# Attention in chunks and an MLP on one Trainium2 core: V, scores and attention output by halves of a tile from the fifth tile on, and the last stores in eight transfers

## The chip, the cores and the metric

The kernel runs on one core of a Trainium2 chip. The metric is the time of one execution on the device in microseconds (us), taken as the median of several runs. A core has several engines that work side by side and wait for each other by semaphores: TensorE (PE in the profile, with PEld for its weight loads), VectorE (DVE), ScalarE (ACT), GpSimd (POOL), and SyncE (SP), which here only issues transfers. Sixteen DMA engines move data between the device's memory and the on-chip memory.

## The reference: what is computed

Eight batches of eight heads with 576 positions of 64 numbers go through attention within chunks of 64 positions, and the result through a two-layer MLP with an exact GELU:

```python
scores = scale * np.matmul(q_c, k_c.transpose(0, 1, 2, 4, 3))   # within each chunk of 64
attn = softmax(scores)                                          # over the 64 keys
out = np.matmul(attn, v_c)
x = out.transpose(0, 2, 1, 3).reshape(4608, 512)
h = x @ w_in                                                    # 512 x 2048
return gelu(h) @ w_out                                          # 2048 x 512
```

## The kernel before, in words

**Tiles.** A batch has nine chunks. The first eight (512 positions, `MT`) of batch t make tile t, for t = 0 to 7. The ninth chunks of all eight batches make a ninth tile, t = 8 (`B` in the code). Each tile has 512 rows of x. A tile goes through loads, casts to bf16 on GpSimd, scores, softmax, attention output (AV), x with the 512 features on the partitions, the first MLP product (`mm1_groups`), and the second (`mm2_seven` from tile 3 on, otherwise `mm2_slot`).

**Order.** The whole order is written out by hand. `phase(t, ...)` runs the MLP of tile t. Into it are hung, at named places (words of a written program in the first product, numbered places in the second), the steps of later tiles: scores of tile t+2 and AV and x of tile t+1 in the second product, and the issue of loads still further ahead. Each engine executes its own queue in that order, and SP's queue holds nearly all loads, all transposes by DMA and all stores but half of the last ones.

**From tile 4 on** (`FIRSTX = 4`) the attention goes as follows.

- `load_v_rows` (L113) loads V as 256-byte runs, one for each key and head, into a tile of 128 partitions x 8 heads x 4 slots. Heads of even and odd number are placed differently: `place(r, i)` (L148) gives for chunk i and head parity r the half of the partitions (0 or 1) and the slot. An even head has chunk i in half i % 2, an odd one in the other half. So a tile of the first eight takes four transfers for the even heads (128 KB each) and five for the odd ones (three of 128 KB and two of 64 KB), and tile 8, whose chunks come from eight batches, takes eight for each parity (64 KB each).
- `cast_v_rows` (L198) casts V on GpSimd in two steps, one for each head parity, into a tile with one more column, which holds ones, so that AV also gives the sums of the softmax.
- `quad_S` (L222) computes the scores: 64 products of 64x64 for a tile. The array of PE works as four quarters; a product occupies a half of the rows (the head parity r) and a half of the columns (o = c ^ r, with c the parity of the chunk). There are four banks of results, one for each pair of head groups and c. ScalarE takes the exponential of each bank.
- `rows_av` (L316) computes AV with the positions on the partitions: 64 products of 64 x 65. They lie in six banks: block b = (head group, pair of chunks) from 0 to 15, seven blocks in a bank, and a bank for each head parity. The sixth bank is borrowed from the second MLP product (`last`, the bank Z).
- `rows_x` (L333) divides on DVE, bank by bank (a reciprocal at L346 and a product at L348), and SP transposes the result into x by DMA, in two pieces (L340): blocks 0 to 6 after the first two banks, blocks 7 to 15 after all six.

**Around it.** `x_blocks` (L593) splits x into four blocks (two halves of the features, two halves of the positions) for a scheme with seven products in place of eight; `x_sums` (L597) makes four differences of them on DVE. In `mm1_groups` (L632) the word `p` stands for a plain block of four products with 512 columns (L685); from tile 3 on only tile 8 has such blocks, four of them.

**Loads around V of the last tiles.** During phase 5 SP issues the first part of tile 7's V, the transposes of x, a store, the second part of tile 7's V, the eight loads of tile 8's queries (L111), a store and the eight loads of tile 8's keys (L106). During phase 6 follow the transposes of tile 8's queries and keys (L187), for which GpSimd's casts (L154) must be done, and V of tile 8.

**The end.** `last_seven` (L794) computes the second product of tile 8. Its first half of the rows is stored by four transfers (two blocks m of 128 rows, two chunks each), its second half by eight (two column halves, two blocks, two chunks). In `store_rows` (L822) the even chunk's store goes out on SP and the odd one's on ScalarE's queue, so each issues six.

## Time and profile before

| | us |
|---|---|
| median of three runs | 272.89 (272.04 to 274.34) |
| profiled execution | 272.8 |
| its span, first to last instruction | 271.0 |
| TensorE busy | 260.0 (96% of the span) |
| VectorE, ScalarE, GpSimd busy | 199.6, 186.7, 76.8 |

The granted clock of TensorE was 0.996 of full speed in the mean over the span. The DMAs moved 56.60 MB at 209 GB/s in the mean. Times in rows of the profile are counted from the start of the span. In a row of a time order the first number is the start and the second the length in us; a bracket at the end gives the idle time of the engine just before and what ended it. The queue of an engine's issues has a q behind its name (SPq, ACTq). A row of a group has the count, the busy time, the mean in ns, and the idle time before it.

### The profile page before, as it was taken

The page shows a single profiled execution, that of the slowest core. Times are in us where ns is not written, and L with a number is a line of the kernel's source. Part 1 is how long each engine was busy: PE and PEld are TensorE (multiplying, and loading weights), DVE is VectorE, ACT ScalarE, POOL GpSimd, SP SyncE. Part 2 cuts the span into 40 slices and gives each one's busy share as a digit, 9 for nine tenths or more (in the row PEclk, how much of TensorE's full clock was granted, in tenths as well). Part 3 has the DMA queues.
Part 4 walks back from the last instruction along what each step waited for, and adds up shares of the span by engine and source line. Part 5 has one row for each costly group of instructions (what it writes and reads, how often), then busy time and mean ns, then how long its engine had stood idle before and what let it go on. Part 6 is the DMA issues. An engine that isn't in the chain of part 4 may idle for free.

```text
span 271.0 us, 7549 instructions
## 1 busy us (share of the span) xinstructions
PE 260.0 (96%) x3063; PEld 194.5 (72%) x3080; DVE 199.6 (74%) x368; ACT 186.7 (69%) x363; POOL 76.8 (28%) x127
## 2 busy tenths in 40 slices
PE   7989999999999999999999999999999999999990
PEld 3454454486458644888888888888888888887780
DVE  2673786979998789599669956985897589756930
ACT  3467756897767968895699579947994797259400
POOL 2635658361351151342036003610132011000000
PEclk9999999999999999999999999999999999999998
DMA  6999999998969998998999999996699560530014
GB/s 203 252 344 405 396 400 242 255 283 208 323 162 210 255 228 196 268 253 126 204 263 233 231 192 257 256 192 153 214 221 194 132 186 20 119 116 2 0 33 126
DMA packets 127523, 56.60 MB, mean 209 GB/s; under 512 B 103936, under 2 KB 121344, under 8 KB 127488
## 3 DMA queue, kind: packets, MB, share of 16 engines
q1 hardware_dynamic: 127008, 55.59, 81.7%
q10 hardware_dynamic: 480, 0.52, 0.8%
q8 instruction: 24, 0.39, 0.6%
q14 instruction: 11, 0.09, 0.1%
HBM read 36.70 MB, written 9.44 MB: 170 GB/s over the span
## 4 chain that ended last, share of the span: by engine, by line
PE 80%; SPq 9%; DMA 5%; issue 1%; POOL 1%; ACT 0%; DVE 0%; POOLq 0%
PE y_ps L730 20%; PE h_Y L663 12%; PE y_ps L844 11%; PE h_Z L663 8%; PE h_X L663 8%; PE h_ps L523 5%; PE y_ps L869 4%; PE y_ps L739 3%; PE h_ps L685 2%; DMA arrival<-in_moe_w_in_dram 2%; SPq L139 2%; SPq L106 2%; SPq L111 2%; PE s_ps L232 2%; DMA k_t<-k_nat 1%
## 5 line engine op out<-in xcount | busy, mean ns | idle before, releaser
L663 PEld LDWEIGHTS <-w_in_s 128*128 128x128 bf16 x464 | 45.3, 98 | 6.1
L663 PEld LDWEIGHTS <-w_in_sb 128*128 128x128 bf16 x348 | 34.0, 98 | 6.8 <-issue 0.5
L154 POOL CAST q_nat<-arrival 128x512 bf16<-128x512 f32 x33 | 19.4, 627 | 47.4 <-DMA arrival<-in_q_dram 47.1
L663 PE MATMUL h_X<-x,w_in_sb 128*128 128x256 bf16 x232 | 32.6, 272 | 0.0
L844 PE MATMUL y_ps<-w_out_sb,h 128*128 128x512 bf16 x137 | 31.7, 379 | 0.9 <-issue 0.8
L730 PEld LDWEIGHTS <-h_s 128*128 128x128 bf16 x304 | 29.7, 98 | 3.4
L663 PE MATMUL h_Y<-x_t,w_in_s 128*128 128x256 bf16 x232 | 31.8, 272 | 0.0
L730 PEld LDWEIGHTS <-h 128*128 128x128 bf16 x288 | 27.9, 98 | 3.6
L206 POOL CAST v_nat<-arrival 128x1024 bf16<-128x1024 f32 x14 | 15.2, 1098 | 50.9 <-DMA arrival<-in_v_dram 50.8
L154 POOL CAST k_nat<-arrival 128x512 bf16<-128x512 f32 x34 | 21.7, 673 | 22.5 <-DMA arrival<-in_k_dram 20.5
L730 PE MATMUL y_ps<-w_t,h_s 128*128 128x256 bf16 x208 | 24.8, 273 | 0.0
L844 PEld LDWEIGHTS <-h 128*128 128x128 bf16 x144 | 13.4, 98 | 15.0 <-issue 0.2
L730 PE MATMUL y_ps<-w_out_sb,h 128*128 128x256 bf16 x192 | 22.9, 273 | 0.0
L941 ACT ACT_TABLE_LOAD x16 | 20.5, 1283 | 1.0 <-PEq L1161 0.7
L670 ACT ACTIVATE h<-h_Y 128x512 bf16<-128x512 f32 x29 | 17.1, 594 | 2.0 <-PE h_Y L663 1.6
L698 ACT COPY h_Y<-h_X 128x512 f32<-128x512 f32 x29 | 16.5, 583 | 2.8 <-PE h_X L663 2.6
L670 ACT ACTIVATE h<-h_X 128x512 bf16<-128x512 f32 x29 | 17.2, 596 | 1.4 <-PE h_X L663 0.8
L663 PE MATMUL h_Z<-x_t,w_in_s 128*128 128x256 bf16 x116 | 17.4, 273 | 0.0
L663 PE MATMUL h_Z<-x_t,w_in_sb 128*128 128x256 bf16 x116 | 16.9, 272 | 0.0
L663 PE MATMUL h_Y<-x,w_in_s 128*128 128x256 bf16 x116 | 16.9, 273 | 0.0
L239 ACT ACTIVATE pT<-s_ps 128x512 bf16<-128x512 f32 x28 | 14.5, 601 | 2.7 <-PE s_ps L232 2.7
L709 DVE COPY h_a<-h_Y 128x512 f32<-128x512 f32 x8 | 5.5, 692 | 14.5 <-PE h_Y L663 14.5
(145 smaller groups left out, 492.0 us busy)
## 6 DMA issues: line engine op xcount, KB each, us to landing
arrival<-in_q_dram SPq DMA_DIRECT2D x7, 1024.0 KB
arrival<-in_k_dram SPq DMA_DIRECT2D x24, 256.0 KB
out_dram<-y_sb SPq DMA_DIRECT2D x22, 256.0 KB
arrival<-in_v_dram SPq DMA_DIRECT2D x42, 128.0 KB
arrival<-in_moe_w_out_dram SPq DMA_DIRECT2D x4, 1024.0 KB
out_dram<-y_sb SPq DMA_DIRECT2D x5, 512.0 KB
arrival<-in_v_dram SPq DMA_DIRECT2D x8, 256.0 KB
arrival<-in_moe_w_in_dram SPq DMA_DIRECT2D x4, 512.0 KB
```

The lines of the kernel that those rows point to most:

```text
L154: copy(st[nm][:, g].rearrange("p j r d -> p r j d"), st[nm + "f"][:, 2 * g:2 * g + 2])
L206: copy(st["v"][:, r::2, :, :D], st["vf"][:, r::2])
L239: nc.scalar.activation(pT[:].rearrange("p u (c j) -> p u c j", j=J), s_ps[g2][c][:].rearrange("p u (j c) -> p u c j", j=J), Act.Exp, scale ...
L523: nc.tensor.matmul(h_ps[a][:], w_in_sb[:, ks, f * P:(f + 1) * P], st["x"][:, ks, :], start=(ks == 0), stop=(ks == KS - 1))
L663: nc.tensor.matmul(banks[g + name][:, i], lhs[:, kk, i], rhs[:, kk], start=fresh and i == kk == 0, stop=(kk == 1), skip_group_check=True)
L670: nc.scalar.activation(h[:, j:j + 2, m], src[:], Act.Gelu)
L698: AC(banks[g + "Y"][:], banks[g + "X"][:])
L730: nc.tensor.matmul(out[m], lhs[:, f, m * P:(m + 1) * P], rhs[:, f, :], start=fresh and f == 0 and (m == 0 or len(out) == 3), stop=(f == FH ...
L739: nc.tensor.matmul(out[m], lhs[:, f, m * P:(m + 1) * P], rhs[:, f, :], start=False, stop=(f == FH - 1), skip_group_check=True)
L844: nc.tensor.matmul(y_ps[:], st["h"][:, f, ms * P:(ms + 1) * P], w_out_sb[:, f, :], start=(f == 0), stop=(f == FF - 1))
L869: nc.tensor.matmul(tiles[t]["y_ps", ms][:], tiles[t]["h"][:, f, ms * P:(ms + 1) * P], w_out_sb[:, f, :], start=(f == 0), stop=False)
L941: nc.scalar.activation(act_scratch[:], rest[:, 0:1], func)
```

## The change

Only tiles 4 to 8 and the last stores are touched.

- V: a new `load_v_halves` loads all heads of a chunk together. `spot(i)` places the chunks: 0 to 3 as before in half i % 2 and slots 0 and 1, chunks 4 to 7 crosswise in the other half, in slots 2 and 3, for all heads alike. A tile of the first eight takes five transfers, two for the first half of the positions (256 KB each) and three for the second (256, 128 and 128 KB); tile 8 takes eight of 128 KB. They are issued at the places where the two parities were.
- The two casts of V go by slots (halves of the positions) in place of head parity.
- Scores: the column half is that of `spot`, the same for both head parities, and the bank goes by the head parity in place of the chunk parity.
- AV: six banks, three for each half of the positions, with 6, 6 and 4 columns of heads; x is divided in that order, and each half is transposed by one DMA of eight blocks when its three banks are done.
- x is stored by halves of the positions; `x_blocks` and the plain blocks of tile 8 read it that way (the latter in two runs of 256 columns).
- The last stores: the first half of the rows takes two transfers in place of four, the right column half two in place of four, the left column half four as before; eight in all, four on each of the two queues. A store then covers two blocks m where it did one.

```diff
@@ -127,11 +127,21 @@
                 go(raw[:, 1::2, n], v[t, 1::2, CH + P * n:CH + P * (n + 1), :])
             go(raw[0:CH, 1::2, last], v[t, 1::2, MT - CH:MT, :])
             go(raw[CH:P, 1::2, last], v[t, 1::2, 0:CH, :])
-        if t == B:
-            for b in range(B):
-                for r in parity:
-                    c, n = place(r, b)
-                    go(raw[CH * c:CH * (c + 1), r::2, n], v[b, r::2, MT:S, :])
+
+    def spot(i):
+
+        return (i % 2, i // 2) if i < CT // 2 else ((i + 1) % 2, 2 if i in (5, 6) else 3)
+
+    def load_v_halves(t, halves=range(2)):
+
+        if "vf" not in tiles[t]:
+            tiles[t]["vf"] = stage_tile()[:].rearrange("p (h n d) -> p h n d", h=H, d=D)
+        for s in halves:
+            runs = [(i, 1) for i in range(4 * s, 4 * s + 4)] if t == B else ([(0, 2), (2, 2)], [(5, 2), (7, 1), (4, 1)])[s]
+            for i, n in runs:
+                o, slot = spot(i)
+                rows = v[i, :, MT:S, :] if t == B else v[t, :, CH * i:CH * (i + n), :]
+                nc.sync.dma_start(tiles[t]["vf"][CH * o:CH * (o + n), :, slot], rows.rearrange("h key d -> key h d"))
 
     def load_v_plain(t):
         tiles[t]["vf"] = stage_tile()[:].rearrange("p (h n d) -> p h n d", h=H, d=D)
@@ -203,7 +213,8 @@
         if t >= FIRSTX:
             nc.gpsimd.memset(st["v"][:, :, :, D:], 1.0)
         for r in range(2):
-            copy(st["v"][:, r::2, :, :D], st["vf"][:, r::2])
+            part = (slice(0, H), slice(2 * r, 2 * r + 2)) if t >= FIRSTX else (slice(r, H, 2), slice(0, CT // 2))
+            copy(st["v"][:, part[0], part[1], :D], st["vf"][:, part[0], part[1]])
 
     def four_banks(name):
         return [[pool.tile([P, CT, CH], f32, tag=tag, name=name) for pool, tag in ((ps_tp, "tp"), (ps_at, "at"))]
@@ -228,8 +239,11 @@
         for g2, u, g, n, r, c, o, rs, os in quadrants():
             if g2 not in pairs:
                 continue
-            i = 2 * n + c
-            nc.tensor.matmul(s_ps[g2][c][os, u, :].rearrange("p (j c) -> p j c", j=J),
+            i, bank = 2 * n + c, c
+            if t >= FIRSTX:
+                o, bank = spot(i)[0], r
+                os = slice(CH * o, CH * (o + 1))
+            nc.tensor.matmul(s_ps[g2][bank][os, u, :].rearrange("p (j c) -> p j c", j=J),
                              st["kt"][rs, g * J + n, CH * c:CH * (c + 1)],
                              st["qt"][rs, g * J:(g + 1) * J, i * PC:(i + 1) * PC],
                              start=True, stop=True, tile_position=(CH * r, CH * o))
@@ -310,45 +324,45 @@
                                 st["rc", 2 * g2 + c][:].rearrange("p (n u) e -> p n e u", u=2),
                                 op=mybir.AluOpType.mult)
 
-    NX = MT // (D + 1)
     FIRSTX = 4
+    NX = 3
+
+    def by_halves(t):
+        return tiles[t]["x"][:].rearrange("p g m -> p (g m)").rearrange("p (s g e) -> p s g e", s=2, g=G)
 
     def rows_av(t, last):
 
         st = tiles[t]
         banks = [pool.tile([P, MT], f32, tag=tag, name="av_ps")
                  for pool, tag in ((ps_tp, "tp"),) * 2 + ((ps_at, "at"),) * 3] + [last]
-        st["av"] = [b[:, :NX * (D + 1)].rearrange("p (i e) -> p i e", e=D + 1) for b in banks]
-        for b in range(G * CT // 2):
-            for c in range(2):
-                for r in range(2):
-                    bank, i = 2 * (b // NX) + r, b % NX
-                    g, n, o = b // (CT // 2), b % (CT // 2), c ^ r
-                    os, cs = slice(CH * o, CH * (o + 1)), slice(CH * c, CH * (c + 1))
-                    nc.tensor.matmul(st["av"][bank][cs, i, :],
-                                     st["pT", 2 * (g // 2) + c][os, CT // 2 * (g % 2) + n, :],
-                                     st["v"][os, 2 * g + r, place(r, 2 * n + c)[1], :],
-                                     start=True, stop=True, tile_position=(CH * o, CH * c))
+        st["av"] = [b[:, :2 * NX * (D + 1)].rearrange("p (i e) -> p i e", e=D + 1) for b in banks]
+        for b in range(G * 2):
+            for r in range(2):
+                for s in range(2):
+                    for c in range(2):
+                        g, n = b // 2, 2 * s + b % 2
+                        o, slot = spot(2 * n + c)
+                        os, cs = slice(CH * o, CH * (o + 1)), slice(CH * c, CH * (c + 1))
+                        nc.tensor.matmul(st["av"][3 * s + b // NX][cs, 2 * (b % NX) + r, :],
+                                         st["pT", 2 * (g // 2) + r][os, CT // 2 * (g % 2) + n, :],
+                                         st["v"][os, 2 * g + r, slot, :],
+                                         start=True, stop=True, tile_position=(CH * o, CH * c))
 
     def rows_x(t):
 
         st = tiles[t]
-        rows = work.tile([P, G * CT // 2, 2, D], bf16, tag="x_t", name="x_r", bufs=1)
-        xT = st["x"][:].rearrange("p g (n e) -> p (g n) e", e=P)
-
-        def flip_rows(b0, b1):
-            nc.sync.dma_start_transpose(xT[:, b0:b1], rows[:, b0:b1].rearrange("p b r d -> p (b r d)"))
+        rows = work.tile([P, 2, 2 * G, 2, D], bf16, tag="x_t", name="x_r", bufs=1)
+        xT = by_halves(t).rearrange("p s g (n e) -> p s (g n) e", e=P)
         for bank in range(6):
-            b0 = NX * (bank // 2)
-            ni = min(NX, G * CT // 2 - b0)
-            av = st["av"][bank][:, :ni]
-            one = work.tile([P, NX], f32, tag="one", name="one", bufs=2)
-            nc.vector.reciprocal(one[:, :ni], av[:, :, D])
-            to = rows[:, b0:b0 + ni, bank % 2]
-            nc.vector.tensor_tensor(to, av[:, :, :D], one[:, :ni].to_broadcast([P, ni, D]), op=mybir.AluOpType.mult)
-            if bank == 1:
-                flip_rows(0, NX)
-        flip_rows(NX, G * CT // 2)
+            s, b0 = bank // 3, NX * (bank % 3)
+            nb = min(NX, 2 * G - b0)
+            av = st["av"][bank][:, :2 * nb]
+            one = work.tile([P, 2 * NX], f32, tag="one", name="one", bufs=2)
+            nc.vector.reciprocal(one[:, :2 * nb], av[:, :, D])
+            nc.vector.tensor_tensor(rows[:, s, b0:b0 + nb].rearrange("p b r d -> p (b r) d"), av[:, :, :D],
+                                    one[:, :2 * nb].to_broadcast([P, 2 * nb, D]), op=mybir.AluOpType.mult)
+            if bank % 3 == 2:
+                nc.sync.dma_start_transpose(xT[:, s], rows[:, s].rearrange("p b r d -> p (b r d)"))
 
     def duo_banks(g2, name):
         pool, tag = ((ps_at, "at"), (ps_tp, "tp"))[g2]
@@ -591,6 +605,9 @@
         TT(s4, a12, s2, op=sub)
 
     def x_blocks(t):
+        if t >= FIRSTX:
+            x = by_halves(t)
+            return x[:, 0, :2], x[:, 1, :2], x[:, 0, 2:], x[:, 1, 2:]
         x = tiles[t]["x"][:].rearrange("p (c k) (n m) -> p c k n m", c=2, n=2)
         return x[:, 0, :, 0], x[:, 0, :, 1], x[:, 1, :, 0], x[:, 1, :, 1]
 
@@ -682,7 +699,9 @@
                 f = plain.pop(0)
                 bank = ps_tp.tile([P, MT], f32, tag="tp", name="h_ps")
                 for ks in range(KS):
-                    nc.tensor.matmul(bank[:], w_in_sb[:, ks, f * P:(f + 1) * P], st["x"][:, ks, :],
+                    nc.tensor.matmul(bank[:].rearrange("p (s e) -> p s e", s=2), w_in_sb[:, ks, f * P:(f + 1) * P],
+                                     by_halves(t)[:, :, ks] if t >= FIRSTX else
+                                     st["x"][:, ks, :].rearrange("p (s e) -> p s e", s=2),
                                      start=(ks == 0), stop=(ks == KS - 1))
                 nc.scalar.activation(st["h"][:, f, :], bank[:], Act.Gelu)
             elif word in hs:
@@ -809,20 +828,24 @@
         W = ps_mm.tile([P, 2, NH], f32, tag="mm", name="y_ps")
         product(halves(W), h_sum(t, 4), w[:, 1, :, 1], True)
         TT(y[0][:, :, NH:], W[:], s5[:], op=add)
-        for m in range(2):
-            store_rows(t, 0, m, y)
+        store_rows(0, slice(0, 2), y)
 
         def row_block(m, nh):
             cols = slice(nh * NH, (nh + 1) * NH)
             TT(y[1][:, m, cols], Zs[m], (s2, s5)[nh][:, m], op=add)
-            store_rows(t, 1, m, y, cols)
+            if nh == 0:
+                store_rows(1, slice(m, m + 1), y, cols)
+            elif m == 1:
+                store_rows(1, slice(0, 2), y, cols)
         product(Zs, h_sum(t, 3), T[3], True, lambda m: row_block(m, 1))
         product(Zs, h[:, 1, :, 1], T[4], False, lambda m: row_block(m, 0))
 
-    def store_rows(t, th, m, y, cols=slice(0, d_model)):
+    def store_rows(th, ms, y, cols=slice(0, d_model)):
+        rows = out.rearrange("(i s) n -> s i n", s=S)[MT:S]
         for c in range(P // CH):
-            m0 = ((th * (TH // P) + m) * (P // CH) + c) * S + MT
-            (nc.sync if c == 0 else nc.scalar).dma_start(out[m0:m0 + CH, cols], y[th][c * CH:(c + 1) * CH, m, cols])
+            i0 = (th * (TH // P) + ms.start) * (P // CH) + c
+            i1 = i0 + (ms.stop - ms.start - 1) * (P // CH) + 1
+            (nc.sync if c == 0 else nc.scalar).dma_start(rows[:, i0:i1:P // CH, cols], y[th][c * CH:(c + 1) * CH, ms, cols])
 
     def store_whole(t, th, y):
         m0 = t * S + th * TH
@@ -1093,7 +1116,7 @@
                     nc.gpsimd.tensor_copy(tiles[4]["q"][:, 0, 0, 0, 0:1], tiles[3]["kt"][:, G * J - 1, 0:1])
                     pool_cast_qk(4)
                     flips_of(4)
-                    load_v_rows(4)
+                    load_v_halves(4)
                     load_qk(5, "q")
                     cast_v_rows(4, PO)
                 e1[f"i{G - 1}"] = [behind_k]
@@ -1103,11 +1126,11 @@
                     if t + 2 < NT:
                         flips_of(t + 2)
                     if t < B - 2:
-                        load_v_rows(t + 2, (0,))
+                        load_v_halves(t + 2, (0,))
                     if t in (FIRST7 + 1, FIRST7 + 2):
                         cast_v_rows(t + 1, PO)
                     if t == B - 1:
-                        load_v_rows(B, (1,))
+                        load_v_halves(B, (1,))
                         cast_v_rows(B, PO)
 
                 def next_q(t=t):
@@ -1121,9 +1144,9 @@
 
                 def rest_of_v(t=t):
                     if t < B - 2:
-                        load_v_rows(t + 2, (1,))
+                        load_v_halves(t + 2, (1,))
                     if t == B - 2:
-                        load_v_rows(B, (0,))
+                        load_v_halves(B, (0,))
                     if t + 3 == B:
                         cast_v_rows(t + 2, PO)
                 e1 = {"begin": [ahead]}
```

## The prediction

> **What bounds the kernel now.** I read the page first, then the busy time by stretches, and then three places in order of time: the one late wait, the queue of SyncE (SP) ahead of it, and the end. Behind the first fence stand the page's own lines, behind the second the stretches (their length, then TensorE's busy time, and so on to the share and rate of the DMAs).
>
> ```profile
> span 271.0 us, 7549 instructions
> PE 260.0 (96%) x3063; PEld 194.5 (72%) x3080; DVE 199.6 (74%) x368; ACT 186.7 (69%) x363; POOL 76.8 (28%) x127
> ```
>
> ```profile
> 0.00:20.00 20.00, 17.01 (x236) 9.28 (x239) 10.50 (x23) 9.39 (x19) 8.70 (x24) 1.00 0.89 264
> 20.00:107.50 87.50, 86.29 (x919) 49.30 (x930) 70.81 (x124) 64.93 (x143) 38.88 (x57) 1.00 0.98 276
> 107.50:199.80 92.30, 92.24 (x1175) 80.73 (x1174) 71.64 (x135) 74.14 (x134) 24.63 (x39) 1.00 0.99 217
> 199.80:214.10 14.30, 13.88 (x242) 12.11 (x241) 10.59 (x24) 9.08 (x16) 2.47 (x5) 1.00 0.97 189
> 214.10:252.60 38.50, 38.37 (x389) 32.34 (x389) 28.22 (x54) 27.31 (x51) 2.09 (x2) 1.00 0.31 85
> 252.60:265.30 12.70, 12.22 (x112) 10.70 (x110) 7.88 (x13) 1.80 (x4) 0.00 (x0) 1.00 0.12 29
> 265.30:271.00 5.70, 0.00 (x0) 0.00 (x0) 0.00 (x0) 0.00 (x0) 0.00 (x0) 0.82 0.49 125
> ```
>
> TensorE (PE) is the bound: 260.0 of 271.0 us. Its 11.0 us of idle time are what a change of transfers can win. The change begins with tile 4, whose V is loaded from 101.12 us on (row below), so the 4.2 us that lie idle before 107.5 are out of reach. Behind that PE misses 0.06 us in 92.3, then 0.42 us between 199.80 and 214.10, 0.13 us up to 252.6, and then the end: 5.70 us in which no engine computes and only the last stores go out. So two places can pay, the 0.42 us and the end. Anything that adds PE time, on the other hand, is paid in full.
>
> **The change, part by part.** *Transfers of V and the late wait.* V of tiles 4 to 7 takes 5 issues on SP in place of 9 (2 and 3 in place of 4 and 5); V of tile 8 takes 8 in place of 16. The bytes and the 256-byte runs stay. The first nine of them, and what an issue costs:
>
> ```profile
> 101.12 5.95 SPq L120 DMA_DIRECT2D arrival<-in_v_dram  x9
> ```
>
> ```profile
> L111 SPq DMA_DIRECT2D arrival<-in_q_dram x8: 596/596/828, 187.3 to 192.0; - x8
> L120 SPq DMA_DIRECT2D arrival<-in_v_dram x70: 462/610/2610, 51.8 to 223.4; - x70
> L102 SPq DMA_DIRECT2D arrival<-in_k_dram x20: 643/1092/4677, 44.7 to 165.1; - x20
> ```
>
> The three numbers are least, median and greatest ns. The new form of 128 rows x 8 heads x 256 bytes is that of K (L102): 0.64 us where the DMAs keep up, 1.09 us at the median. Between 0.60 us (128 runs, L111) and 0.64 us (1024 runs) the size hardly counts, so the price is per issue. The place where it matters is the load of tile 8:
>
> ```profile
> 177.21 2.23 SPq L120 DMA_DIRECT2D arrival<-in_v_dram  x4
> 179.55 2.67 SPq L340 DMA_TRANSPOSE x<-x_r  x2
> 184.21 3.05 SPq L120 DMA_DIRECT2D arrival<-in_v_dram  x5
> 187.30 5.35 SPq L111 DMA_DIRECT2D arrival<-in_q_dram  x8
> 193.21 6.87 SPq L106 DMA_DIRECT2D arrival<-in_k_dram  x8
> 186.94 0.75 DVE L607 TENSOR_TENSOR x_t<-x 128x512 bf16<-128x512 bf16 x2
> 202.59 2.29 POOL L154 CAST k_nat<-arrival 128x512 bf16<-128x512 f32 x4 [4.28 <-DMA arrival<-in_k_dram]
> 204.91 1.76 SPq L187 DMA_TRANSPOSE k_t<-k_nat  x1
> 208.92 0.74 PE L232 MATMUL s_ps<-q_t,k_t 64*64 64x64 bf16 x64 [0.41 <-DMA k_t<-k_nat]
> ```
>
> ```profile
> POOL q_nat L1134 <- DVE h_s L562: 5.5, 1, 5.5
> ```
>
> SP issues without a break from 184.21 to 200.1; the last keys land, GpSimd casts them, they are transposed, and PE waits 0.41 us for them. Three issues in place of five ahead of this chain cost 3 x 0.64 = 1.9 us in place of 3.05 (with the median of 1.09, for the one full-height transfer and 0.61 for the two others, 2.3 us): the chain starts 0.7 to 1.1 us sooner, more than the 0.41 us. I take **-0.41 us**. Nothing is late next: the cast of tile 8's queries, ahead of the keys', waits 5.5 us for DVE's h_s (last row), not for a load, and is over before the keys come. Were the DMAs themselves late, it is 0. Elsewhere the saved issues are covered by PE, which waits for no load behind 107.5 us; without that cover they would be worth at most 24 x 0.6 us of SP, so they can only help.
>
> *Halves in GpSimd's cast, DVE and the transposes of x.* One cast holds 1024 elements a row before and after, and its only new condition is that it waits for all of a half's transfers, as it did. DVE's rows:
>
> ```profile
> L348 DVE TENSOR_TENSOR x_r<-av_ps,one 128x448 bf16<-128x448 f32 x20 | 12.5, 624 | 0.7
> L348 DVE TENSOR_TENSOR x_r<-av_ps,one 128x128 bf16<-128x128 f32 x5 | 1.5, 291 | 0.2
> ```
>
> From these two sizes an element costs (624 - 291) / 320 = 1.04 ns. New banks hold 384, 384, 256 twice: 2 x (557 + 557 + 424) = 3.08 us, against 4 x 624 + 2 x 291 = 3.08 us. So **0**. The first transpose on SP waits for three banks in place of two, about 0.4 us later on DVE; SP reaches it later than that anyway (179.55 us above, and the fewer issues in front only bring it to the wait), and the second waits for the last bank as before. Both are issued by 182.22 us, and the sums of x begin at 186.94 us, 4.7 us behind. The sizes 8 and 8 in place of 7 and 9 blocks count nothing. The four plain blocks of tile 8 read x in two runs of 256 in place of one of 512; a run of 256 is what the products read all along, so 0.
>
> *Scores and AV on PE.* Both keep 64 products a tile; what changes is the order in which the four quarters of the array are used, and in the scores the bank. Row half and column half of the old scores go (0,0) (1,1) (0,1) (1,0): a diagonal step, then one within a column. The new ones go (0,0) (1,0) (0,1) (1,1): the same two kinds. The old AV took only steps within a column or a row; the new one takes diagonals and steps within a row, as the AV of tiles 1 to 3 does. The rows (start, us on the chain, count):
>
> ```profile
> 128.86 0.67 PE s_ps L232 x64
> 71.00 0.67 PE av_ps L301 x64
> 228.26 0.59 PE av_ps L328 x57
> 228.97 1.91 PE y_ps L739 x16
> 41.17 0.45 PE L371 MATMUL s_ps<-qT,kT 64*64 64x64 bf16 x32
> 104.08 0.45 PE L232 MATMUL s_ps<-q_t,k_t 64*64 64x64 bf16 x32
> ```
>
> Scores stay at 0.67 us. AV of 65 columns took 228.97 - 228.26 = 0.71 us and should take 0.67 x 65/64 = 0.68: between 0 and -0.15 us over five tiles, and I take **0**. A bank for each row half (new scores) against one for each chunk parity (old) is no difference either: tile 1 has the former (L371) and tile 4 the latter (L232), both 0.45 us for 32. Here the Trainium skill speaks (TensorEngine Tiling (Array Packing), Restrictions and Gotchas): different row tiles cannot access one PSUM bank at the same time. By that rule the old scores, with both row halves in one bank, would run two by two and the new ones four by four, a gain that stands among the rivals; the two rows of 0.45 us do not bear it out.
>
> *The last stores.* 12 become 8, on SP and on ScalarE's queue in turn, 6 to 4 on each.
>
> ```profile
> 264.86 0.42 DVE L817 TENSOR_TENSOR y_sb<-y_ps,y 128x256 f32<-128x256 f32 x1 [0.45 <-PE y_ps L730]
> 262.12 3.77 SPq L825 DMA_DIRECT2D out_dram<-y_sb  x6
> 262.41 2.43 ACTq L825 DMA_DIRECT2D out_dram<-y_sb  x1
> 264.88 2.61 ACTq L825 DMA_DIRECT2D out_dram<-y_sb  x4
> 267.58 0.55 ACTq L825 DMA_DIRECT2D out_dram<-y_sb  x1
> ```
>
> ```profile
> 266.00:267.00 1.00, 0.00 (x0) 0.00 (x0) 0.00 (x0) 0.00 (x0) 0.00 (x0) 1.00 0.98 273
> 267.00:268.00 1.00, 0.00 (x0) 0.00 (x0) 0.00 (x0) 0.00 (x0) 0.00 (x0) 1.00 0.55 154
> 268.00:269.00 1.00, 0.00 (x0) 0.00 (x0) 0.00 (x0) 0.00 (x0) 0.00 (x0) 0.97 0.45 108
> 269.00:270.00 1.00, 0.00 (x0) 0.00 (x0) 0.00 (x0) 0.00 (x0) 0.00 (x0) 0.50 0.10 24
> ```
>
> The last sum is there at 265.28. SP is done at 265.89, but ScalarE's queue only at 267.58 + 0.55 = 268.13: its first store took 2.43 us, and the other five follow at (267.58 - 264.88) / 4 = 0.675 us each. So the end is set by issues on ScalarE's queue, not by the rate: the DMAs fall from 273 to 108 GB/s while it still issues. New: the first store ends at 264.84 again (I keep its 2.43 us, a price of the first one on this queue, since SP's six took 3.77 us, 0.63 each), and the last of three more starts at 264.88 + 2 x 0.675 = 266.23: **-1.35 us**. All data are there by then. Bounds: 0 where bytes set the end; -2.24 us where the first store costs no more than the others and ScalarE ends with SP (268.13 - 265.89); and +1.1 us where the 2.43 us grow with the store, which is twice as large (+2.43 - 1.35).
>
> **Sum.** The profiled execution took 272.8 us, 1.8 us around its span of 271.0, and the median of the three runs is 272.89. 272.8 - 0.41 - 1.35 = 271.04, so **271.0 us**, 0.7% under the median. About 1% is what a measurement of this kernel can tell from no change.
>
> **The rivals.** (a) *Slower: the quarters get in each other's way.* Place: the new scores, whose neighbours share a column half, on PE's chain. If they ran two by two, 0.67 us more for each of tiles 4 to 8: 272.8 + 3.35 - 1.76 = 274.4; if one by one, three times 0.67 each, 281.1. It decides from 0.35 us a tile (1.76 / 5). Against it: each kind of step stands in a row above, with no more than 0.04 us between them.
> (b) *The end is set by bytes, the stores' number does not matter*, the gain is the late wait alone: 272.8 - 0.41 = 272.4. For it: the DMAs move 273 GB/s in one us of the end; against it the 108 and 24 behind that. The Trainium skill stands here (DMA: Bandwidth & Descriptors, Issuing engines are not separate DMA queues): issue time is usually small beside the transfer itself.
> (c) *The keys stay late* because the DMAs, not SP, are behind (a share of 0.97 in that stretch): 272.8 - 1.35 = 271.45.
> (d) *The first store on ScalarE's queue gets cheap*, since fewer are issued on SP beside it: 272.8 - 0.41 - 2.24 = 270.15.
> (e) *It grows with the size*: 272.8 - 0.41 + 1.1 = 273.5.
> (f) *Old scores were held up by shared banks* and now take half: 0.33 us x 5 less, 269.4.
>
> **How the numbers follow.** Chances: the forecast 0.50, (a) 0.06, (b) 0.16, (c) 0.12, (d) 0.10, (e) 0.04, (f) 0.02. The range goes from 269.9 (the forecast with the largest gain at the end, and AV's 0.15 us) to 272.9 (b, and half a us for the spread of the runs); outside lie (a), (e), (f), and a little of each of the others. Faster by over 1% means under 270.2 us: about half of (d), and (f), 0.08. Slower by over 1% means over 275.6: (a) beyond two by two, and a wait that no row shows, 0.06. Within 1%: 0.86.
>
> **What would show it.** In the new profile: PE busy within 0.3 us of 260.0; no wait for k_t at tile 8's scores and the keys' cast about 1 us sooner, beside PE's own clock; 0.67 us for 64 scores and about 0.68 us for AV; ScalarE's four stores ending 1.5 us behind the last sum, and the span ending 2.9 us behind them as before (271.0 - 268.1). I am wrong where the first store on ScalarE's queue does not take 2.4 us, or where the span ends as late with eight stores, or where scores lengthen.

## The result, and the profile after

The changed kernel took 272.14 us in the median of 20 runs, the kernel before, measured beside it, 274.05 us. The ratio is 0.9933 with a 95% interval of 0.9912 to 0.9955: 0.7% less time. That is the size that was forecast (272.89 to 271.0), but not by the steps that were forecast. The profiled execution took 271.71 us, 2.1 us of them around its span.

Lines of the changed kernel have other numbers: L825 (the last stores) is now L848, L607 (sums of x) L624, L154 (cast of queries and keys) L164, L206 (cast of V) L217, L712 (combinations of products) L731. First the page's own lines, then three of the stretches.

```profile
span 269.6 us, 7526 instructions
PE 260.6 (97%) x3080; PEld 193.8 (72%) x3080; DVE 201.8 (75%) x368; ACT 186.8 (69%) x363; POOL 78.8 (29%) x127
```

```profile
107.50:199.80 92.30, 91.72 (x1169) 79.89 (x1167) 73.38 (x135) 73.57 (x133) 25.69 (x40) 1.00 0.98 221
199.80:213.70 13.90, 13.86 (x242) 12.15 (x241) 11.55 (x23) 10.00 (x17) 3.66 (x5) 1.00 0.80 178
264.90:269.60 4.70, 0.34 (x4) 0.06 (x1) 0.42 (x1) 0.00 (x0) 0.00 (x0) 1.00 0.60 179
```

The span is 1.4 us shorter, and TensorE is still the bound. From 199.80 on it now misses 0.04 us where it missed 0.42, but in the 92.3 us ahead it misses 0.58 us where it missed 0.06. VectorE is busy 2.2 us longer and GpSimd 2.0 us, although neither has more to do.

**The end.** The last stores of the changed kernel, by their source line (least, median, greatest ns, then first and last start), and the last sum:

```profile
L848 SPq DMA_DIRECT2D out_dram<-y_sb x4: 618/703/737, 262.5 to 265.7; - x4
L848 ACTq DMA_DIRECT2D out_dram<-y_sb x4: 660/759/777, 262.6 to 265.7; - x4
265.28 0.42 DVE L835 TENSOR_TENSOR y_sb<-y_ps,y 128x256 f32<-128x256 f32 x1 [0.45 <-PE y_ps L749]
```

The first store on ScalarE's queue did not take 2.43 us; none there took more than 0.78. The last one starts at 265.7, as soon as the last sum is there (265.28 + 0.42 = 265.70), and the span ends 3.9 us behind that sum. Before it was 271.0 - 265.28 = 5.7 us. So the end gained 1.8 us.

**The late wait.** SP's queue and GpSimd's cast of tile 8's keys in the changed kernel:

```profile
182.25 3.29 SPq L144 DMA_DIRECT2D arrival<-in_v_dram  x3
185.58 5.38 SPq L111 DMA_DIRECT2D arrival<-in_q_dram  x8
191.52 7.05 SPq L106 DMA_DIRECT2D arrival<-in_k_dram  x8
201.09 3.47 POOL L164 CAST k_nat<-arrival 128x512 bf16<-128x512 f32 x4 [1.85 <-DMA arrival<-in_k_dram]
```

The issue of the keys starts at 191.52 in place of 193.21 and their cast at 201.09 in place of 202.59, and no row of PE's waits names k_t any more. TensorE's last product nevertheless ends 0.43 us later than before (the last sum, right behind it, at 265.28 in place of 264.86).

**Where that went.** 0.26 us of it are there already at tile 3's first MLP product (108.66 in place of 108.40), where only the first loads of V differ; that moment varies by 2.8 us over the profiles here (last section), so these 0.26 us may be chance. Behind that, two new waits of PE take the place of the old one. GpSimd's and VectorE's work around them, in order of time, after:

```profile
168.52 2.67 POOL L164 CAST k_nat<-arrival 128x512 bf16<-128x512 f32 x4 [1.90 <-DMA arrival<-in_k_dram]
168.72 0.69 DVE L575 TENSOR_TENSOR h_s<-h 128x512 bf16<-128x512 bf16 x1
169.45 0.71 DVE L576 TENSOR_TENSOR h_s<-h_s,h 128x512 bf16<-128x512 bf16 x1
...
173.00 0.60 PE L680 MATMUL h_Z<-x_t,w_in_sb 128*128 128x256 bf16 x4 [0.21 <-DVE h_d L731]
...
181.22 1.13 POOL L217 CAST v_nat<-arrival 128x1024 bf16<-128x1024 f32 x1 [7.80 <-DMA arrival<-in_v_dram]
181.37 2.06 DVE L584 TENSOR_TENSOR h_s<-h,h_s 128x2048 bf16<-128x2048 bf16 x1
...
187.89 1.23 POOL L217 CAST v_nat<-arrival 128x1024 bf16<-128x1024 f32 x1 [5.54 <-DMA arrival<-in_v_dram]
188.13 1.73 DVE L624 TENSOR_TENSOR x_t<-x,x_t 128x512 bf16<-128x512 bf16 x2
189.45 0.61 PE L680 MATMUL h_Y<-x_t,w_in_s 128*128 128x256 bf16 x4 [0.23 <-DVE x_t L624]
```

The same before:

```profile
168.51 0.41 DVE L561 TENSOR_TENSOR h_s<-h 128x512 bf16<-128x512 bf16 x1
168.96 0.42 DVE L562 TENSOR_TENSOR h_s<-h_s,h 128x512 bf16<-128x512 bf16 x1
169.10 2.44 POOL L154 CAST k_nat<-arrival 128x512 bf16<-128x512 f32 x4 [1.62 <-DMA arrival<-in_k_dram]
...
180.87 1.22 DVE L570 TENSOR_TENSOR h_s<-h,h_s 128x2048 bf16<-128x2048 bf16 x1
182.04 1.04 POOL L206 CAST v_nat<-arrival 128x1024 bf16<-128x1024 f32 x1 [8.30 <-DMA arrival<-in_v_dram]
...
187.61 0.88 DVE L607 TENSOR_TENSOR x_t<-x,x_t 128x512 bf16<-128x512 bf16 x2
189.27 1.05 POOL L206 CAST v_nat<-arrival 128x1024 bf16<-128x1024 f32 x1 [6.19 <-DMA arrival<-in_v_dram]
```

Before, each cast began when VectorE's sums were done or nearly so. Now the loads land sooner, the casts begin 0.6 to 1.4 us sooner, and VectorE's sums of bf16 data lie beside them: 0.69 and 0.71 us in place of 0.41 and 0.42, 2.06 in place of 1.22, 1.73 for two in place of 0.88. TensorE waits 0.21 us behind the first of these places and 0.23 us behind the last, 0.44 together, as much as the late wait had cost. These are single executions; which of the three places belong to the change, the runs below tell. The Trainium skill has this rule (SBUF — State Buffer, Who interferes with whom): a VectorE instruction with two inputs in SBUF contends with a GpSimd instruction that reads there, and whichever starts second is blocked until the other is done. The rows agree in the main: the sum at 181.37 began 0.15 us behind the cast, which ended at 182.35, 0.98 us later, and the sum took 0.84 us longer than its 1.22.

**Scores and AV** in TensorE's order of time, first before, then after:

```profile
128.79 0.74 PE L232 MATMUL s_ps<-q_t,k_t 64*64 64x64 bf16 x64
228.19 0.66 PE L328 MATMUL av_ps<-v_nat,pT 64*64 64x65 bf16 x57
...
228.97 1.91 PE L739 MATMUL y_ps<-w_t,h_s 128*128 128x256 bf16 x16
```

```profile
128.99 0.74 PE L246 MATMUL s_ps<-q_t,k_t 64*64 64x64 bf16 x64
228.63 0.60 PE L346 MATMUL av_ps<-v_nat,pT 64*64 64x65 bf16 x50
...
229.41 1.91 PE L758 MATMUL y_ps<-w_t,h_s 128*128 128x256 bf16 x16
```

The 64 scores take 0.74 us from their first start to their last end in both, and from the first product of AV to the next work it is 0.78 us in both. The new quarters and banks change nothing in these times.

### The profile page after: what moved, and what is told of

Read it like the earlier page. It is cut to its first block, busy times and chain, and to the rows that moved or that the text cites. A ratio compares the mean times of both kernels' runs of the same rounds, so it can differ in the third digit from the quotient of the medians.

```text
span 269.6 us, 7526 instructions
## 1 busy us (share of the span) xinstructions
PE 260.6 (97%) x3080; PEld 193.8 (72%) x3080; DVE 201.8 (75%) x368; ACT 186.8 (69%) x363; POOL 78.8 (29%) x127
## 4 chain that ended last, share of the span: by engine, by line
PE 67%; SPq 11%; DMA 10%; POOL 4%; DVE 2%; issue 2%; ACT 1%; POOLq 0%; ACTq 0%; DVEq 0%
PE y_ps L749 24%; PE h_Y L680 11%; PE h_Z L680 8%; PE h_X L680 7%; PE y_ps L867 6%; SPq L120 5%; DMA arrival<-in_moe_w_out_dram 5%; PE h_ps L537 4%; PE y_ps L758 4%; DMA arrival<-in_moe_w_in_dram 2%; SPq L149 2%; DMA k_u<-k_nat 2%; SPq L108 2%; PE s_ps L246 2%; POOL w_out_sb L948 1%
## 5 line engine op out<-in xcount | busy, mean ns | idle before, releaser
L867 PE MATMUL y_ps<-w_out_sb,h 128*128 128x512 bf16 x144 | 33.0, 380 | 0.0
L164 POOL CAST q_nat<-arrival 128x512 bf16<-128x512 f32 x33 | 19.7, 638 | 43.1 <-DMA arrival<-in_q_dram 42.9
L164 POOL CAST k_nat<-arrival 128x512 bf16<-128x512 f32 x34 | 23.1, 716 | 20.9 <-DMA arrival<-in_k_dram 16.8
L217 POOL CAST v_nat<-arrival 128x1024 bf16<-128x1024 f32 x14 | 15.1, 1088 | 46.7 <-DMA arrival<-in_v_dram 46.6
```

The source lines that it names most:

```text
L164: copy(st[nm][:, g].rearrange("p j r d -> p r j d"), st[nm + "f"][:, 2 * g:2 * g + 2])
L217: copy(st["v"][:, part[0], part[1], :D], st["vf"][:, part[0], part[1]])
L867: nc.tensor.matmul(y_ps[:], st["h"][:, f, ms * P:(ms + 1) * P], w_out_sb[:, f, :], start=(f == 0), stop=(f == FF - 1))
```

## The experiments

The theory as it stood at first: the end gains by the number of stores, the late wait by the number of issues on SP. The rival: the first store on ScalarE's queue is cheap for a reason of its own, and the number of stores hardly counts. Ratios are to the kernel before on the same chip, with 95% intervals. "The end" is the time from the last sum to the end of the span, in the profiled execution.

**Part by part.** e1 is the kernel before with the diff's part on the last stores alone; e2 is the changed kernel with the old stores; e3 is the kernel before, once more.

```diff
 e1 (before, the calls of the last stores as changed)
-            store_rows(t, 1, m, y, cols)
+            if nh == 0:
+                store_rows(1, slice(m, m + 1), y, cols)
+            elif m == 1:
+                store_rows(1, slice(0, 2), y, cols)
 e2 (after): the reverse, here and at the calls for the first half
```

> The kernel before with one part of the change, the last stores in eight transfers in place of twelve. Theory (the gain is made at the end, on ScalarE's queue, which issues four stores in place of six): 1.3 to 1.9 us less than before, the span ends about 4.3 us behind TensorE's last product in place of 6.2, and the wait for the transposed keys of tile 8 (0.41 us) stays. Rival (the gain comes from V's fewer transfers and the bytes set the end): less than 0.4 us less than before, and the span still ends about 6 us behind the last product.

> The changed kernel with its last stores put back to twelve. Theory: within 0.5 us of before, the end again 5.7 to 6.2 us behind TensorE's last product; the wait for tile 8's keys is gone (-0.4 us), and about as much is lost where GpSimd's cast of V, which now comes sooner, lies beside the sums of x on VectorE. Rival: 1.4 to 1.9 us less than before, the end 4.3 us behind the last product.

> The kernel before, unchanged, for a second profile. It tells what in the first profile belongs to the kernel and what to the one execution. If the 2.43 us of the first store on ScalarE's queue belong to the twelve stores, it is again over 2 us, and the queue ends about 2.9 us behind the last sum; if it was chance, it is 0.6 to 0.8 us and the queue ends about 1 to 1.5 us behind. The wait for tile 8's keys should be there again, 0.2 to 0.6 us.

```profile
L829 ACTq DMA_DIRECT2D out_dram<-y_sb x4: 607/796/2620, 262.1 to 266.5; - x4
```

```profile
L844 ACTq DMA_DIRECT2D out_dram<-y_sb x6: 473/576/607, 263.1 to 267.2; - x6
```

```profile
L825 ACTq DMA_DIRECT2D out_dram<-y_sb x6: 553/582/2467, 262.2 to 267.4; - x6
```

The rows are of e1, e2 and e3: the greatest of the three durations is that of the first store. It takes 2.6 us with four stores on each queue (e1) and 0.6 us with six (e2). So the price went with the part on V, which does not touch a store, and neither the number of stores nor SP's issues beside it decide. e1: end 4.9 us, ratio 0.9945 [0.9913, 0.9978]; e2: end 4.0 us, 0.9939 [0.9909, 0.9969]; e3: 272.62 us, end 5.8 us. Both expectations failed in part: e1's time fell as expected, but it ends 5.4 us behind the last product and not 4.3, and e2, expected near the kernel before, gained 1.7 us, as its rival said. Neither e1 nor e3 has a wait of PE for k_t, although V is loaded there as before. So the late wait of 0.41 us is not a fixed property of that kernel either.

**More stores.** e4 is the kernel before with sixteen last stores, the first half of the rows by column halves too.

```diff
         for m in range(2):
-            store_rows(t, 0, m, y)
+            for nh in range(2):
+                store_rows(t, 0, m, y, slice(nh * NH, (nh + 1) * NH))
```

> The kernel before with sixteen last stores: the first half of the rows by column halves too, so eight stores on each queue. Theory (the number of stores on ScalarE's queue sets the end): its last store starts 2 x 0.675 = 1.35 us later than in the profile before, and the span ends 7 to 7.6 us behind the last product. Rival (bytes set the end): 6.2 us behind it as before, since the bytes are the same.

```profile
L826 ACTq DMA_DIRECT2D out_dram<-y_sb x8: 496/565/2155, 258.3 to 266.0; - x8
```

One execution took 271.09 us, with an end of 4.2 us, 1.5 us less than with twelve stores: neither the theory nor its rival. The price (2.2 us) is still paid, but at 258.3, while TensorE works. So the number of stores does not set the end; a stall shortly ahead of it does.

**What the price hangs on.** In the program's listing of ScalarE's instructions, counted from 0, its first last store is number 448 in the kernel before, in e1, e3 and e4, and number 447 in the changed kernel and in e2. The traces agree: counted among ScalarE's records in order of time, the first last store is one place earlier than in the listing, 447 in the kernel before and 446 in the changed one, which has one semaphore wait less ahead of a copy into y_sb at 151.8 us (L774 before). In the DMA view of the 2.5 us from the first store on, an instruction fetch (queue q14) shows in the kernel before and none in the changed one (in the runs below, e6 and e10 have one there again, and e2 and e5 none):

```profile
q1 hardware_dynamic: 215, 0.32, 53.5%
q14 instruction: 1, 0.01, 1.3%
```

```profile
q1 hardware_dynamic: 111, 0.23, 43.6%
```

The fetch is not gone, though: both pages count eleven on q14, and the changed kernel has one at 266.43 us, beside its last store. New theory: the store stalls because a block of ScalarE's instructions ends right there. Rival: the halves of V disturb less, by their time or their queue. One instruction more, far from the end, tells them apart: the table of exponentials is selected a second time at the start of the program. e5 is that edit on the kernel before (number 449), e6 on the changed kernel (448), e9 on e1 (449), e10 on e2 (448); e12 is e5 once more.

```diff
         act_table(Act.Exp)
+        act_table(Act.Exp)
         keep_warm(7)
```

> The kernel before with one tiny activation more on ScalarE at the very start (0.2 us), so that every later instruction of ScalarE stands one place further back: its first store is instruction 449 in place of 448, counted from 0, and a wait of 4.2 us stands at 448. In the profiles so far the 2 us price of the first store is there in every kernel in which it is instruction 448 (before twice, eight stores, sixteen stores) and gone in both in which it is 447, and with it goes a fetch of 8 KB on the queue of instructions, 0.3 to 0.7 us behind the store's start. Theory (the store waits for its own instruction's block to be fetched, and the change moved it by one place): the first store takes 0.5 to 0.8 us, twelve stores as before, the span ends about 4.0 us behind the last sum in place of 5.7, and the time is 1.3 to 2.2 us less than before. Rival (the price belongs to V's placing and transfers, or is that of the queue's first store in the old order): 2.4 us again, the time as before.

> The changed kernel with the same tiny activation more at the start: the first store on ScalarE's queue becomes instruction 448 again. Theory (place in the instruction stream): the first store takes 2.2 to 2.7 us, the span ends about 5 us behind the last sum, as with eight stores in the old kernel, and 1 us of the gain is lost: 0.6 to 1.2 us less than before remain. Rival: the first store takes 0.8 us, the end stays 3.9 us behind the last sum.

> The kernel before with eight last stores and ScalarE's instructions shifted by one (first store at 449). With the runs so far this fills the table of three factors: eight stores, V's part, and the first store off place 448. Theory from the profiles' ends (5.7 us behind the last sum before; 5.0 with eight stores; 4.2 with twelve and no price; 3.9 with both): first store 0.5 to 0.8 us, the end 3.8 to 4.1 us behind the last sum, 1.2 to 2.2 us less than before. Rival (the first store's price is an effect of the profile and costs little in the timed runs, where the number of stores decides): as with eight stores alone, whatever the shift; the two differ by less than 0.4 us.

> The changed kernel with twelve last stores and ScalarE's instructions shifted by one (first store at 448 again): V's part alone, with the price. Theory: first store 2.2 to 2.7 us, the end 5.4 to 5.9 us behind the last sum, and the time within 0.6 us of before. Rival (V's part gains by itself in timed runs, by early keys): 1 us or more less than before, whatever the end.

> The kernel before, shifted by one instruction on ScalarE, timed again, since its first timing (0.5 us less than before, from 1.6 less to 0.5 more) left open whether the 1.5 us that its profile shows at the end are gained in timed runs. Theory: 1 to 2 us less than before. Rival (the price is not paid, or less, in timed runs): under 0.6 us less again.

The stores on ScalarE's queue of e5, e6, e9 and e10 in turn:

```profile
L825 ACTq DMA_DIRECT2D out_dram<-y_sb x6: 473/572/844, 262.3 to 266.2; - x6
```

```profile
L848 ACTq DMA_DIRECT2D out_dram<-y_sb x4: 621/722/2501, 261.7 to 265.8; - x4
```

```profile
L829 ACTq DMA_DIRECT2D out_dram<-y_sb x4: 656/746/774, 264.8 to 268.0; - x4
```

```profile
L844 ACTq DMA_DIRECT2D out_dram<-y_sb x6: 552/584/2570, 263.5 to 268.7; - x6
```

The price goes and comes with that one instruction, in all four pairs. Over all runs here the first store took 2155 to 2620 ns at number 448 (before, e1, e3, e4, e6, e10) and 572 to 742 ns in the eight others, where it is number 447 or 449 (446 in e7, by the trace). So the place of the first store decides, and the rival is out. But the place alone is not enough: in e2 the second store on ScalarE's queue is number 448, and it took 0.58 us, behind a pause of 0.32 us:

```profile
263.98 0.58 ACTq L844 DMA_DIRECT2D out_dram<-y_sb  x1
```

The four corners, with the ends of the profiled executions and the timed ratios:

| | twelve stores | eight stores |
|---|---|---|
| first store at 448: end | 5.7 before, 5.8 e3, 5.5 e10 | 4.9 e1, 4.4 e6 |
| else: end | 4.2 e5, 4.1 e12, 4.0 e2 | 3.9 after, 4.2 e9 |
| old V, at 448: ratio | 1 | 0.9945 [0.9913, 0.9978] e1 |
| old V, else | 0.998 [0.9943, 1.0017] e5; 0.9905 [0.9876, 0.9934] e12 | 0.9929 [0.99, 0.9958] e9 |
| V in halves, at 448 | 0.9966 [0.9943, 0.9989] e10 | 0.9946 [0.9907, 0.9984] e6 |
| V in halves, else | 0.9939 [0.9909, 0.9969] e2 | 0.9933 [0.9912, 0.9955] after |

By the ends, in the mean of each corner, eight stores are worth 5.67 - 4.64 = 1.0 us while the price is paid and less than 0.1 us (4.09 to 4.06) without it; the price is worth 1.6 us with twelve stores and 0.6 us with eight. The two overlap: both shorten the same queue. The timed ratios say the same less sharply, and four of the five expectations were missed in time: e5 gained 0.5 us and, timed again as e12, 2.6 us (1.3 to 2.2 and 1 to 2 were expected), e6 kept 1.5 us of the gain (0.6 to 1.2), e10 0.9 us (under 0.6); only e9, with 1.9 us, came out as expected. Averaged over the other two factors (the two timings of one kernel taken as one, 0.9943), without the price it is 0.9936 against 0.9964, about 0.8 us; with eight stores 0.9938 against 0.9962, about 0.65 us; with V in halves 0.9946 against 0.9954, about 0.2 us. A single cell is uncertain by 0.2 to 0.4%, and e5 and e12, one kernel on two chips, differ by 0.75%, more than their intervals allow. So the order of these shares is shown by the ends; their sizes in the timed runs are not settled.

**The issues on SP.** e7 is the changed kernel with the second half of tile 7's V in twelve transfers of two heads in place of three, ahead of tile 8's keys on SP's queue.

```diff
-                nc.sync.dma_start(tiles[t]["vf"][CH * o:CH * (o + n), :, slot], rows.rearrange("h key d -> key h d"))
+                parts = 4 if t == B - 1 and s == 1 else 1
+                for h0 in range(0, H, H // parts):
+                    hs = slice(h0, h0 + H // parts)
+                    nc.sync.dma_start(tiles[t]["vf"][CH * o:CH * (o + n), hs, slot], rows[hs].rearrange("h key d -> key h d"))
```

> The changed kernel with the second half of tile 7's V in twelve transfers in place of three, of two heads each: the same bytes, nine more issues on SP ahead of the loads of tile 8's queries and keys. Theory of the late wait (SP's issues at 0.6 us each decide when the keys come): SP is done with the keys about 9 x 0.6 = 5.4 us later, and TensorE waits 3.5 to 5.5 us for the transposed keys at tile 8's scores. Rival (the DMAs' rate decides): the keys come at most 1 us later, and TensorE waits under 1 us.

```profile
183.72 8.11 SPq L147 DMA_DIRECT2D arrival<-in_v_dram  x12
191.88 5.22 SPq L111 DMA_DIRECT2D arrival<-in_q_dram  x8
197.66 9.12 SPq L106 DMA_DIRECT2D arrival<-in_k_dram  x8
209.15 3.58 POOL L167 CAST k_nat<-arrival 128x512 bf16<-128x512 f32 x4 [5.30 <-DMA arrival<-in_k_dram]
```

```profile
PE s_ps L249 <- DMA k_t<-k_nat: 6.0, 1, 6.0
```

One execution took 281.72 us. The same bytes by nine issues more take 4.8 us more of SP (8.11 against 3.29), the keys' cast starts 8.1 us later than in the changed kernel, and TensorE waits 6.0 us, somewhat more than expected. Of the 8.1 us, 1.5 are this execution's later start (110.19 against 108.66 us at tile 3's first MLP product), and the issue of the keys took 2.1 us longer (9.12 against 7.05), for which no cause is shown. So more issues ahead of the keys make them late, and rival (c), by which fewer issues would not help, is out. As to its size: with the old V the wait was 0.41, 0, 0, 1.0, 0.5, 0 and 1.2 us (before, e3, e1, e4, e5, e12, e9), 0.44 in the mean; with V in halves it was 0 in each of after, e2, e6, e8, e10, e11.

**What gives it back.** e8 is the changed kernel with GpSimd's casts of tile 7's V behind the sums of x, by a copy of one column of their result; e11 is the same kernel, timed.

```diff
-                    if t + 3 == B:
-                        cast_v_rows(t + 2, PO)
...
-                    e2[4] += [next_k]
+                    e2[4] += [lambda t=t: cast_v_rows(t + 2, PO, tiles[t + 1]["T"][4][:, 0, 0:1]), next_k]
```

> The changed kernel with both casts of tile 7's V on GpSimd put behind the four sums of x of tile 6 (the cast waits for the last of them). Theory (VectorE's operations on bf16 take longer where a cast of GpSimd lies beside them): at this place the sums of x take 0.40 to 0.43 us each and the fourth sum of h 1.22 us, as where GpSimd is idle, in place of up to 1.27 and 2.06 us, and TensorE has no wait for the sums of x. Rival (the slow sums have another cause, such as x itself being late): they stay long, or the wait stays.

> The changed kernel with tile 7's casts behind the sums of x, as in the one look before, now timed. Theory: the change's own gain and 0.2 to 0.6 us more where a cast lay beside VectorE's sums: 1.8 to 2.8 us less than before. Rival: the casts' place makes no difference beyond the spread of the runs, 1.2 to 2.4 us less than before like the change itself.

Rows of e8 in order of time:

```profile
181.19 1.22 DVE L584 TENSOR_TENSOR h_s<-h,h_s 128x2048 bf16<-128x2048 bf16 x1
...
187.95 0.88 DVE L624 TENSOR_TENSOR x_t<-x,x_t 128x512 bf16<-128x512 bf16 x2
...
189.24 2.04 POOL L217 CAST v_nat<-arrival 128x1024 bf16<-128x1024 f32 x2
```

The sums take their old 1.22 and 0.88 us, PE has no wait behind 107.5 us that a view would list, and e8's one execution took 271.07 us. The casts of the keys were not moved, and in e11's profile 0.4 us of PE's wait for h_d are back. Timed, e11 has 0.9895 [0.986, 0.993]: less than the kernel before, and 2.9 us where 1.8 to 2.8 were expected; against the changed kernel (0.9933 [0.9912, 0.9955]) the intervals overlap.

How much of this belongs to the change, all fourteen profiles tell. One of the four sums of x takes 1.18 to 1.27 us in place of 0.42 in after, e2, e6 and e10, and none does in e7, where the second half of V comes late, nor in e8 and e11, where the cast stands behind the sums. With the old V one does in e1 alone of seven profiles (the row has two sums, 0.88 us where nothing lies beside them):

```profile
187.74 1.60 DVE L607 TENSOR_TENSOR x_t<-x,x_t 128x512 bf16<-128x512 bf16 x2
187.88 1.19 POOL L206 CAST v_nat<-arrival 128x1024 bf16<-128x1024 f32 x1 [4.76 <-DMA arrival<-in_v_dram]
```

So the stretched sums of x come of the cast beside them, and the change makes that meeting the rule. The 2.06 us at 181.37 stand in the changed kernel's own profile alone; in e6 that sum began 0.45 us ahead of the cast and kept its 1.22 us, while the cast took 1.68 in place of 1.04. And the sums of h beside the keys' cast are stretched in the kernel before as well (0.75 us in e3), and e1 has a wait of 0.4 us for h_d: that place was a draw, not the change.

## Why the prediction was right, and where it was not

- **The total** was right, 0.7% less, but two errors in it cancel. Of the 1.76 us predicted, the end gave 1.8 by itself (1.35 were predicted), and TensorE's last product came 0.43 us later where 0.41 us sooner was predicted. With 0.3 us more around the span the profiled execution gained 1.1 us. That the errors cancel is luck. (Two slips do not matter: the low end of the range comes out at 270.0, not 269.9, and half of (d) with (f) at 0.07, not 0.08.)
- **The step that failed** is "the first store ends at 264.84 again (I keep its 2.43 us, a price of the first one on this queue ...)". It is no price of every first store, but of a first store at place 448 in ScalarE's list of instructions: elsewhere it took 572 to 742 ns. The changed kernel left that place by chance. With the price kept, the -1.35 us is the right kind of step: e1 and e6 ended 4.9 and 4.4 us behind the last sum, 0.8 and 1.4 us less than before. Without it the stores' number is worth less than 0.1 us, not 0.675 each: the last issue then starts at the last sum, and only its own 0.78 us and the landing follow. Why the place has this effect stays open.
- **Rival (d)**, the cheap first store, is what happened, but its reason ("since fewer are issued on SP beside it") is refuted by e1 and e2. It gave no 2.24 us since the last store cannot start ahead of the last sum. (b), by which the number of stores does not matter, holds without the price (4.09 against 4.06 us) and fails with it (5.67 against 4.64).
- **The late wait** was right in kind: with three issues for five the keys' cast starts 1.5 us sooner (0.7 to 1.1 predicted), and nine more make 6.0 us of wait. Its 0.41 us was one draw between 0 and 1.2.
- **"So 0" for the casts** looked only at what each cast costs and waits for. It left out that loads that land sooner move the casts, and that a cast beside VectorE's sums stretches them: 0.44 us of new waits in this profile, of which the 0.23 us for the sums of x go with the change. The cover of those casts was VectorE's pause behind the sums, and I did not name it.
- **Scores, AV, divisions, transposes, plain blocks** at 0 were right: 0.74 and 0.78 us as before; the products of the divisions take the 557 and 424 ns that were worked out, a transpose 1.31 us in the median before and after, and a product of a plain block 379 ns before and after. Rivals (a) and (f) are out.
- **TensorE's busy time** is 260.6, not within 0.3 of 260.0; but the trace of before has 3063 products on record and that of after 3080, so this compares records, not work.

## What to carry to other kernels

A duration that only one instruction in a queue shows (2.43 us where its neighbours take 0.6) is to be explained before it is kept or dropped in a sum; here one instruction more at the start of the program was the test that told. When loads get faster, follow the casts behind them: what they will run beside is part of the price. And a small wait in one trace (0.41 us) is one draw; a second profile of the same kernel showed 0.

## What the runs showed of the hardware

- **The first store on ScalarE's queue took 1.4 to 2.0 us longer where it was ScalarE's instruction 448** (2155 to 2620 ns in six profiles, 572 to 742 in the eight where it was another). One instruction more or less far ahead of it switched this. The page of the changed kernel has two kinds of fetches:

```profile
q8 instruction: 24, 0.39, 0.7%
q14 instruction: 11, 0.09, 0.1%
```

  0.39 MB in 24 are 16 KB each, 0.09 MB in 11 about 8 KB. The Trainium skill (Runtime: NRT & Kernel Launch, Instruction fetch mechanics) describes blocks of 16 KiB and says that crossing a border is mostly hidden. The fetches of 8 KB on q14 are smaller, and there the measurement decides. That 448 is a border is suggested, not shown: in the kernel before, fetches on q14 begin at 119.56, 187.35 and 261.42 us, when VectorE has started 193, 320 and 448 of its records, about 128 apart; and one begins 0.4 to 0.9 us behind the start of each of the six slow stores. Why the second store of e2, also number 448, took 0.58 us, and the wait at 448 in e5 cost nothing at the end, stays open.
- **Sums of bf16 data on VectorE took up to twice as long beside a cast on GpSimd that had begun first** (0.88 to 1.73 us for two, 1.22 to 2.06 for one); in e6, where the sum began first, the cast took 1.68 us in place of 1.04.
- **The time up to the first MLP product of tile 3 varied** from execution to execution by 2.8 us (107.4 to 110.2 us over the profiles here), more than the whole effect of the change, and with no visible relation to the edits.
